# The expert planner of an attention and mixture-of-experts kernel: VectorE's runs on the port shared with GpSimd enter the plan, and the due times are set anew

## The chip, the cores and the metric

One core of a Trainium2 chip. The metric is the device time of one execution in microseconds. Of three runs of the kernel before, the median is 1438.96 us (1438.61 to 1439.52). The profiled execution took 1439.4 us; its span, from the first to the last instruction, is 1437.7 us.

## The reference, cut to what matters

```
scores = q @ k^T / 8                          # 8 batches x 8 heads, 576 x 576, head size 64
keep the 32 largest of each row, softmax, @ v
x = the heads side by side                    # 4608 tokens x 512
logits = x @ w_gate                           # 4608 x 8 experts
for (token, expert) in order of falling logit:
    if token has no expert and expert holds < 576: assign
for each expert e: out[tokens of e] = relu(x @ w1[e]) @ w2[e]    # 512 -> 1024 -> 512
```

Each expert ends with exactly 576 tokens. Which 576 they are is only known when the logits of all tokens are there, so the expert part begins when the attention part has ended.

## The kernel before, in words

`attention` (up to L455) computes x and the logits L, `moe` (L571) the rest. After it comes a check of flags (`redo`), which computes again only what a cheap test finds doubtful; here nothing is computed again.

The expert part handles the experts one after the other, in an order that the data decide: the expert that fills up first is `p` = 0, and so on. For each `p` there are five pieces of work:

- `route(p)` (L637): finds the expert that fills first among those left, and the logit at which it is full. VectorE masks the logits and finds each free token's best expert (L642 to L650). Then six steps: compare all tokens with 32 thresholds (g, L663, in three pieces), count the hits by matmul (L669), fold the counts (cm L673, ch L676), sum (L680), compare with 576 (ok L682), sum (L683), take the highest threshold (mx L688) and make the next thresholds (L694, L695). At the end ei, the expert's number (L699), the positions of its tokens, and, in a chain of its own (L734 to L736), the penalty `pen` and the list U of free tokens that the next routing needs.
- `enlist(p)` (L737): turns the positions into a list of 576 token numbers, idx (L778).
- `weigh(p)` (L779): SyncE loads the expert's w1 and w2 (four transfers of 1 MB, ring of four buffers). They are split into two f16 parts: ScalarE makes the high part in eight chunks (L802), VectorE the rest in sixteen halves, w1l and w2l (L810). There are two sets of split weights.
- `bring(p)` (L825): GpSimd gathers the 576 rows of x by five indirect DMAs (L832), ScalarE and VectorE split each piece into xs (L852, L855), SyncE transposes it into xT (L856). For `p` = 0 TensorE transposes instead (L842). There are two xT buffers and four buffers for gathered rows.
- `ffn(p)` (L857): 16 groups of 12 matmuls for the first product (L872), relu on ScalarE (hh, L881) and its remainder on VectorE (hl, L882); then 108 matmuls of the second product (L896, L899), copies to ob (L906, L908, L910), and five scatters by indirect DMA on GpSimd (L911).

Besides these, `verdict` (L913) does the cheap test: some dozen VectorE instructions on the statistics of the attention part and one matmul.

The order of the instructions on each engine's queue is not the order of this list. Each operation is entered in a `Plan` (L21) with its engine (V, A, G, P for TensorE, D for SyncE's DMA queue), what it waits for, a planned duration `d`, a time `late` from its end to its result, and a due time `t`. `Plan.run` then plays the work through on planned clocks: on each engine, of the operations that could start within `window` of the first that can, it takes the one with the smallest `t`, and among the engines the one that starts first. The instructions are written to the queues in that order, and the chip works each queue strictly in that order, with the waits that the dependences need.

The due times of the expert part are offsets to 47 per expert, in the dictionary at L583: RT is subtracted for `route`, TE added for `enlist` after the routing's end (TE0 for `p` = 0), TN for the chain of `pen` and U, WT and XT are subtracted for weights and x (WT0, XT0 for `p` = 0), WD is the step from one weight chunk to the next, RA and RD are those of relu and its remainder, VD is the verdict's. The `W_` entries are the windows of the engines. `GL` is the planned time from a gather's end to its rows' arrival.

The attention part is ordered by another instance of the same class, with due times and windows of its own (L140).

Of the kernel before, what the change touches and what calls it, by code (L numbers as in the profile page):

```python
# [7 lines left out]
F32 = mybir.dt.float32  # L8
# [12 lines left out]
class Plan:  # L21
# [11 lines left out]

    def at(self, t, f, pre=(), take=None, free=(), e=None, d=0.0, late=0.0, order=(), m=0):

        pre, order = ([p for p in l or () if p is not None] for l in (pre, order))
        op = dict(t=t, f=f, n=len(pre) + len(order), next=[], pre=pre, order=order, take=take, left=0, free=[], e=e, d=d, late=late, m=m)
# [12 lines left out]
    def run(self):  # L50
        clock = {e: 0.0 for e in "VAGPD"}
        ready = {e: [] for e in clock}
        count = mode = 0

        def add(op):
# [6 lines left out]
        def go(op, start):  # L62
            nonlocal count, mode
# [507 lines left out]
def moe(tc, K, L, x, w1, w2, out, marks=None):  # L571
# [4 lines left out]
    with ExitStack() as ctx:  # L576
# [26 lines left out]
        def span(c):  # L603

            Lf=L.rearrange("p t e -> p (t e)")
            def a0():
                R["rng"]=sm.tile([128,2],F32,name="rng"); V.tensor_reduce(R["rng"][:,0:1],Lf,axis=AX.X,op=ALU.min)
            c.add("V",.37,a0)
            c.add("V",.37,lambda: V.tensor_reduce(R["rng"][:,1:2],Lf,axis=AX.X,op=ALU.max))
            c.add("V",.07,lambda: V.tensor_scalar(R["rng"][:,0:1],R["rng"][:,0:1],-1.0,None,op0=ALU.mult))  # L610
# [26 lines left out]
        def route(p,c):  # L637
# [7 lines left out]
            c.add("V",.37,lambda: V.tensor_reduce(o("v",128,NT),D_["ml"],axis=AX.X,op=ALU.max))  # L645
            c.add("V",.37,lambda: V.tensor_tensor(o("oh",128,NT,E),D_["ml"],D_["v"].unsqueeze(2).to_broadcast([128,NT,E]),op=ALU.is_equal))
            c.add("V",.37,lambda: V.tensor_tensor(D_["oh"],D_["oh"],rev.unsqueeze(1).to_broadcast([128,NT,E]),op=ALU.mult))
            c.add("V",.37,lambda: V.tensor_reduce(o("ce",128,NT),D_["oh"],axis=AX.X,op=ALU.max))
            if p: c.add("V",.11,lambda: V.tensor_tensor(D_["ce"],D_["ce"],U,op=ALU.mult))
            c.add("V",.37,lambda: V.tensor_tensor(o("ohb",128,NT,E,dt=BF16),D_["ce"].unsqueeze(2).to_broadcast([128,NT,E]),rev.unsqueeze(1).to_broadcast([128,NT,E]),op=ALU.is_equal))  # L650
            if p<E-1:
                pcs=3 if p==0 else GP; n=NT//pcs
                D_["lo"]=lo0; D_["thr"]=thr0; lowop=None
                for s in range(STEPS):
# [4 lines left out]
                    for q in range(pcs):  # L659
# [10 lines left out]
                        mms.append(plan.at(c.t,count,cv+(mms[-1:]),e="P",d=.026*(n//4) if p else .03*n+.03,m=0 if p else 32))  # L670
                    c.pre=[mms[-1]]; c.t+=.15
                    if p:
                        c.add("V",.10,lambda: V.tensor_tensor(o("cm",128,32),D_["pc"][:,:32],dm,op=ALU.mult))  # L673
# [3 lines left out]
                        c.add("V",.10,fold)  # L677
# [4 lines left out]
                        c.add("V",.07,lambda: V.tensor_scalar(o("ok",128,E,dt=BF16),D_["pn"][:,:E],float(CAP),-1.0/T,op0=ALU.is_ge,op1=ALU.add))  # L682
                        c.add("P",.04,lambda: P.matmul(D_["pn"][:,16:16+E],quart,D_["ok"],start=True,stop=True,skip_group_check=True))  # L683
                    else:
                        def enough(s=s): D_["okb"]=okbs[s%2]; V.tensor_scalar(D_["okb"][:T,:],D_["pn"][:T,:E],float(CAP),None,op0=ALU.is_ge)
                        c.add("V",.07,enough)
                        c.add("P",.04,lambda: P.matmul(D_["pn"][:,16:16+E],onesb[:T+1,:],D_["okb"],start=True,stop=True,skip_group_check=True),m=33)
                    c.add("V",.07,lambda: V.tensor_reduce(o("mx",128,1,bufs=3),D_["pn"][:,16:16+E],axis=AX.X,op=ALU.max),lowop)  # L688
                    st=stp[:,s:s+1]
# [47 lines left out]
        def enlist(p,c):  # L737
# [29 lines left out]
            c.pre=last  # L767
            c.add("V",.25,lambda: V.tensor_tensor(o("oz",128,4,40),D_["po"][:,:160].rearrange("p (j c) -> p j c",j=4),d4.unsqueeze(2).to_broadcast([128,4,40]),op=ALU.mult))
# [3 lines left out]
            c.add("V",.25,gathered)  # L772
            def spread():
# [51 lines left out]
        def bring(p,t):  # L825
# [31 lines left out]
        def ffn(p,t):  # L857
# [3 lines left out]
            for hf in range(2):  # L861
                for f in range(8):
# [18 lines left out]
                    a=plan.at(t+k_*1.45+RA,lambda B=B,f=f,cs=cs: A.activation(e["hh"][0][:,f,cs],B["ph"][:,:288],AF.Relu),[prev],e="A",d=.291)  # L881
                    e["hl"].append(plan.at(t+k_*1.45+RD,lambda B=B,f=f,cs=cs: V.scalar_tensor_tensor(e["hh"][1][:,f,cs],B["ph"][:,:288],0.0,e["hh"][0][:,f,cs],op0=ALU.max,op1=ALU.subtract),[a],e="V",d=.37,free=[tp]))  # L882
            e["lastx"]=prev; plan.frees(prev,e["txT"])
            t2=t+23.2; i_=0
            for j in ((0,1,4,2,3) if JO else range(5)):
# [23 lines left out]
                a=plan.at(t2+i_*.64,put,[prev],e="A",d=.51,take="ob",free=[tp] if j<4 else None); to=a  # L909
                if j==4: a=plan.at(t2+i_*.64+.1,lambda B=B: V.scalar_tensor_tensor(B["ob"][:64],B["po"][:64],OSC,B["o2"],op0=ALU.mult,op1=ALU.add),[a],e="V",d=.6,free=[tp])  # L910
                plan.at(t2+i_*.64+.2,lambda B=B,j=j,n=n: G.indirect_dma_start(out=out,out_offset=bass.IndirectOffsetOnAxis(ap=D_["idx"][:n,j:j+1],axis=0),in_=B["ob"][:n],in_offset=None),[a],e="G",d=1.04,free=[to],late=2.0)  # L911
            plan.frees(prev,e["tW"]); e["mm"]=prev; e["last2"]=prev
        def verdict(c,acc,cuts,flags):  # L913
# [17 lines left out]
            def total():  # L931
                D_=R["pv"]=new(ps,[128,512],F32,"pl",1); P.matmul(D_[:1,:npr+1],onesf[:,0:1],good[:,:npr+1],start=True,stop=True)
            c.add("P",.11,total)
            c.add("V",.1,lambda: V.tensor_tensor(bad[:,:npr+1],want[:,:npr+1],R["pv"][:1,:npr+1],op=ALU.subtract))
            c.add("V",.1,lambda: V.tensor_scalar(bad[:,:npr],bad[:,:npr],bad[:,npr:npr+1],None,op0=ALU.add))
# [59 lines left out]
```

## Time and profile before

| | |
|---|---|
| median of three runs | 1438.96 us |
| profiled execution | 1439.4 us |
| its span | 1437.7 us |
| TensorE busy | 1274.9 us, 89% |
| VectorE busy | 1207.4 us, 84% |
| GpSimd busy | 884.8 us, 62% |
| ScalarE busy | 864.3 us, 60% |
| mean granted TensorE clock | 0.963 of 2.4 GHz |

Times in the rows further down are microseconds from the span's start. PE is TensorE, DVE VectorE, ACT ScalarE, POOL GpSimd, SP SyncE. A row of the timeline has the start, the duration, engine, line, operation, result and source, and in brackets how long the engine was idle before it and what ended the wait. "x5" means that five equal instructions in a row are merged. The granted clock is a share of full speed: 1.00 is 2.4 GHz, 0.50 is 1.2 GHz, and a stretch's value is a mean.

### The profile page before, as it was taken

What the parts mean: (1) busy time and instruction counts of PE and PEld (TensorE: products, weight loads), DVE (VectorE), ACT (ScalarE), POOL (GpSimd) and SP (SyncE); (2) the same over time, 40 slices, a digit from 0 to 9 for tenths busy, and PEclk for the clock granted to TensorE, in tenths of its full rate; (3) what the DMA queues carried; (4) which work ended last, traced back from release to release, by engine and by line L of the source; (5) the groups of instructions that cost most, each with busy time, mean ns of one, the idle gap of its engine ahead of it and who ended that gap; (6) DMA issues with size and microseconds to landing.
All of it is one profiled execution on the core that took longest, in us unless ns stands there. A gap on an engine that the chain in (4) does not pass through costs nothing.

```text
span 1437.7 us, 41210 instructions
## 1 busy us (share of the span) xinstructions
PE 1274.9 (89%) x14803; PEld 907.1 (63%) x14804; DVE 1207.4 (84%) x6007; ACT 864.3 (60%) x1898; POOL 884.8 (62%) x1286
## 2 busy tenths in 40 slices
PE   2889999999999999999999999955989989998996
PEld 1666776776767677776766777643664664664662
DVE  5899999999999999999999999768978878877620
ACT  2677777777777777787777878713334334335420
POOL 5687888798799789879879888601114224223101
PEclk8899999999999999999999999965999999999998
DMA  5434444544345444463445443004347347349411
GB/s 124 89 87 78 111 99 84 109 79 103 78 112 94 87 115 82 89 120 84 87 115 91 80 117 63 13 34 150 132 99 202 125 93 208 132 92 287 115 33 36
DMA packets 293383, 148.45 MB, mean 103 GB/s; under 512 B 250672, under 2 KB 275248, under 8 KB 292144
## 3 DMA queue, kind: packets, MB, share of 16 engines
q1 hardware_dynamic: 287280, 126.84, 38.7%
q0 software_dynamic: 5888, 18.88, 4.2%
q8 instruction: 118, 1.93, 0.6%
q14 instruction: 97, 0.79, 0.2%
HBM read 71.34 MB, written 18.87 MB: 63 GB/s over the span
## 4 chain that ended last, share of the span: by engine, by line
PE 52%; DVE 30%; DMA 7%; ACT 5%; issue 3%; POOL 2%; SPq 0%; ACTq 0%; POOLq 0%; DVEq 0%
PE ph L872 13%; PE pv L367 9%; DVE cd L223 9%; PE s L238 8%; PE s L220 6%; DVE st L242 5%; PE po L896 4%; DMA xg<-x,idx 3%; ACT w L235 3%; PE pt L289 2%; PE pt L288 2%; PE pt L283 2%; DVE s L241 2%; DMA xT<-xs 2%; DVE cd L227 2%
## 5 line engine op out<-in xcount | busy, mean ns | idle before, releaser
L223 DVE MAX8 cd<-s 128x8 f32<-128x96 f32 x1728 | 373.6, 252 | 34.3 <-PE s L220 29.7
L299 POOL TENSOR_TENSOR elm<-F,ehm 128x512 f16<-128x512 f32 x256 | 294.3, 1156 | 8.0
L245 ACT ACTIVATE r<-s,st 128x576 bf16<-128x576 f32 x288 | 212.9, 739 | 106.8 <-PE s L238 71.5
L235 ACT ACTIVATE w<-s,st 128x576 uint16<-128x576 f32 x288 | 213.2, 740 | 80.2 <-DVE st L231 77.2
L911 POOL DMA_INDIRECT out_dram<-ob,idx x40 | 59.5, 1486 | 288.7 <-ACT ob L906 224.8
L242 DVE MAX8 st<-s 128x8 f32<-128x584 f32 x288 | 220.8, 767 | 7.5 <-PE s L238 2.6
L220 PE MATMUL s<-K,Q 128*128 128x512 f16 (+3 forms) x1280 | 193.0, 291 | 27.6 <-DMA Q<-nq 20.1
L872 PE MATMUL ph<-xT,w1h 128*128 128x288 f16 x1024 | 196.2, 289 | 5.4 <-DMA xT<-xs 5.4
L289 PE MATMUL pt<-Q,K 66*128 66x128 f16 (+1 forms) x1280 | 179.1, 216 | 0.0
L288 PE MATMUL pt<-Q,K 128*128 128x128 f16 (+1 forms) x1280 | 178.5, 215 | 0.0
L296 POOL TENSOR_SCALAR ehm<-F 128x512 f16<-128x512 f32 x256 | 156.5, 617 | 32.5 <-ACT F L293 30.1
L220 PEld LDWEIGHTS <-Q 128*128 128x128 f16 (+1 forms) x1280 | 104.8, 103 | 108.2 <-DMA Q<-nq 19.7
L238 PE MATMUL s<-w,off 128*128 128x512 f16 x576 | 132.7, 288 | 38.5 <-DVE s L241 30.3
L293 ACT ACTIVATE F<-pt 128x512 f32<-128x512 f32 x256 | 150.6, 596 | 14.7 <-PE pt L289 7.9
L872 PE MATMUL ph<-xT,w1l 128*128 128x288 f16 x512 | 148.0, 289 | 0.0
L367 PE MATMUL pv<-vt,E 128*64 128x65 f32 (+1 forms) x1024 | 146.8, 257 | 0.3 <-DVE L L418 0.3
L881 ACT ACTIVATE hh<-ph 128x288 f16<-128x288 f32 x128 | 52.5, 410 | 142.1 <-PE ph L872 126.4
L238 PE MATMUL s<-w,back 128*128 128x512 f16 x576 | 118.9, 288 | 20.6 <-DVE st L242 18.3
L288 PEld LDWEIGHTS <-K 128*128 128x128 f16 x1280 | 117.2, 99 | 18.4 <-issue 5.3
L367 PEld LDWEIGHTS <-ehm 128*128 128x128 f16 x2048 | 115.9, 101 | 9.8
L367 PEld LDWEIGHTS pv<-vt,E 128*64 128x64 f32 (+1 forms) x1024 | 113.2, 164 | 13.5 <-issue 3.1
L367 PE MATMUL pv<-vl,ehm 128*128 128x65 f16 x1024 | 120.8, 193 | 0.0
(267 smaller groups left out, 3281.2 us busy)
## 6 DMA issues: line engine op xcount, KB each, us to landing
wr<-in_moe_w_dram SPq DMA_DIRECT2D x32, 1024.0 KB, 8.3
kn<-in_k_dram SPq DMA_DIRECT2D x64, 128.0 KB, 2.4
qn<-in_q_dram SPq DMA_DIRECT2D x64, 128.0 KB, 2.3
vn<-in_v_dram SPq DMA_DIRECT2D x64, 128.0 KB, 2.3
x<-xb SPq DMA_DIRECT2D x8, 1024.0 KB, 4.4
Q<-nq SPq DMA_TRANSPOSE x160, 3.2
kn<-in_k_dram SPq DMA_DIRECT2D x64, 16.0 KB, 2.3
qn<-in_q_dram SPq DMA_DIRECT2D x64, 16.0 KB, 2.1
```

The source lines that it names most:

```text
L220: T.matmul(s_ps[rows,a:b_],P[Q][:,qc],P[K][:,h*576+a:h*576+b_],start=(Q=="Q1"),stop=(Q=="Q2"))
L223: V.max(D["cd"][:,c*8:c*8+8],D["s"][:,576*c//NCH:576*(c+1)//NCH])
L235: A.activation(D["w"],D["s"][:,:576],AF.Sign,bias=P["st"][:,i,32:33],scale=(1+2.0**-21),accum_out=acc[:,col])
L238: T.matmul(D["s"][:,a:b_],by,w[:,a:b_],start=False,stop=True,skip_group_check=True)
L242: def next8(): V.max(P["st"][:,i,24:32],D["s"][:,:584])
L245: A.activation(r,D["s"][:,:576],AF.Relu,bias=P["st"][:,i,31:32],scale=-1.0)
L288: T.matmul(o,K2[:,kb:kb+128],Q1[:,qc],start=False,stop=False,skip_group_check=True)
L289: T.matmul(o,K3[0:66,kb:kb+128],Q2[0:66,qc],start=False,stop=(c==3 and h==sub[-1][0]),skip_group_check=True)
L296: G.tensor_scalar(D["eh"],D["E"],1.0,0.0,op0=ALU.mult,op1=ALU.add)
L299: G.tensor_tensor(el,D["E"],D["eh"],op=ALU.subtract); P["e"][i]=(D["eh"],el)
L367: for m_ in (range(N-1) if part==0 else (N-1,)): T.matmul(out,seq[m_][0],seq[m_][1],start=(m_==0),stop=(m_==N-1))
L872: P.matmul(B["ph"][:,:288],a[:,c,fs],xT[:,b+c,cs],start=(i==0),stop=(i==11))
```

## The change: what it does

Each operation gets a mark `k`: for a VectorE operation, that it uses the SBUF port which VectorE and GpSimd share (true unless set to 0), for a GpSimd operation, that it needs this port (only set for gathers and scatters). The plan keeps `held`, the time at which VectorE's present run on the port ends. A VectorE operation with the mark, or a short one that follows a run closely, extends it. A marked GpSimd operation is planned to start no earlier than `held`. Operations that read PSUM (hl, ob of the short piece, the counts and sums of the routing, the x pieces of `p` = 0) and the reductions get `k=0`; the weight halves, xs, the comparisons g and the rest keep the mark.

Gathers and scatters are planned with 1.25 in place of 1.04, counting with 0.031 in place of 0.026 per four, one PSUM operation with 0.33 in place of 0.25. The verdict's matmul takes its PSUM buffer from the ring `ph` by way of the plan, where it had the buffer `pl` of its own accord. All due times and windows of the expert part are set anew. No instruction is added or removed.

```diff
+    def at(self, t, f, pre=(), ..., m=0, k=None):
...
+        op = dict(..., k=(e == "V") if k is None else k)
...
+        held = 0.0
...
             if op["e"] == "P" and op["m"] != mode: d, mode = d + self.SW, op["m"]
+            if op["e"] == "V" and (op["k"] or (d < 0.3 and start < held + 0.03)): held = start + d
...
+                    if e == "G" and op["k"]: t = max(t, held)
                     can.append((t, op["t"], op))
...
-        O=dict(RT=57.787, TE=29.172, TN=157.485, WT=10.39, XT=280.745, RD=-10.792, GL=2.6, W_V=0.1079, W_A=1.7878, W_G=21213.0764, W_P=0.0, W_D=0.0257, WD0=53.661, WD1=52.071, RA=146.279, WT0=-182.776, TE0=-21.804, XT0=-92.95, VD=388.103)
+        O=dict(RT=1076.532, TE=-466.322, TN=-392.603, WT=381.255, XT=184.721, RD=-1511.888, GL=2.3, W_V=0.1032, W_A=0.1345, W_G=1000.0, W_P=0.0, W_D=56.256, WD0=988.41, WD1=120.646, RA=-141.446, WT0=130.349, TE0=43.583, XT0=-126.197, VD=3177.794)
...
-                        mms.append(plan.at(..., d=.026*(n//4) if p else .03*n+.03, ...))
+                        mms.append(plan.at(..., d=.031*(n//4) if p else .03*n+.03, ...))
...
-                g=plan.at(t+.1*j,lambda j=j: gather(j),[e["idx"]],e="G",d=1.04,take="xg",late=GL,order=[g,prev])
+                g=plan.at(t+.1*j,lambda j=j: gather(j),[e["idx"]],e="G",d=1.25,take="xg",late=GL,order=[g,prev],k=1)
...
-                    e["x"].append(plan.at(t+.1*j+.03,lo,[a],e="V",d=.6,free=[tp]))
+                    e["x"].append(plan.at(t+.1*j+.03,lo,[a],e="V",d=.6,free=[tp],k=0))
...
-                plan.at(t2+i_*.64+.2, <scatter j>, [a],e="G",d=1.04,free=[to],late=2.0)
+                plan.at(t2+i_*.64+.2, <scatter j>, [a],e="G",d=1.25,free=[to],late=2.0,k=1)
...
-                D_=R["pv"]=new(ps,[128,512],F32,"pl",1); P.matmul(...)
-            c.add("P",.11,total)
+                D_=R["pv"]=new(ps,[128,512],F32,"ph",4); P.matmul(...)
+            tv=c.add("P",.11,total,take="ph",m=1)
```

## Rows read from the trace of the kernel before

**Rows 1.** The page's first part: TensorE's busy time, share, instructions.
```profile
PE 1274.9 (89%) x14803; PEld 907.1 (63%) x14804; DVE 1207.4 (84%) x6007; ACT 864.3 (60%) x1898; POOL 884.8 (62%) x1286
```

**Rows 2.** Busy time by stretch, cut at each expert's first L872; granted clock, DMA.
```profile
core 0: us, PE busy (x) PEld busy (x) DVE busy (x) ACT busy (x) POOL busy (x), PEclk, DMA share, GB/s
...
946.50:995.85 49.35, 18.05 (x280) 14.16 (x281) 42.47 (x153) 9.80 (x11) 7.18 (x5) 0.50 0.32 110
995.85:1053.76 57.91, 53.90 (x400) 33.01 (x399) 49.30 (x155) 20.54 (x36) 12.50 (x9) 0.94 0.40 119
1053.76:1109.42 55.66, 51.86 (x395) 31.80 (x395) 46.66 (x150) 20.32 (x36) 14.98 (x10) 0.97 0.54 150
1109.42:1163.47 54.05, 50.19 (x397) 31.60 (x397) 45.41 (x144) 20.78 (x35) 15.78 (x9) 1.00 0.47 140
1163.47:1217.94 54.47, 51.51 (x397) 32.02 (x397) 45.36 (x144) 20.26 (x34) 17.98 (x11) 0.97 0.49 143
1217.94:1272.05 54.11, 51.59 (x398) 32.06 (x398) 45.42 (x144) 19.86 (x34) 16.30 (x10) 0.97 0.50 143
1272.05:1326.12 54.07, 49.35 (x380) 31.39 (x380) 42.67 (x143) 20.85 (x36) 12.58 (x10) 0.98 0.58 183
1326.12:1376.18 50.06, 50.06 (x325) 31.02 (x326) 28.53 (x62) 19.25 (x33) 11.95 (x11) 0.95 0.47 122
1376.18:1423.40 47.22, 47.22 (x313) 29.27 (x311) 8.01 (x17) 9.54 (x21) 4.74 (x5) 1.00 0.08 27
```

**Rows 3.** TensorE's timeline: the first matmuls of experts 6 and 7.
```profile
1326.12 0.64 PE L872 MATMUL ph<-xT,w1h 128*128 128x288 f16 x2 [4.72 <-DMA xT<-xs]
...
1376.18 0.41 PE L872 MATMUL ph<-xT,w1h 128*128 128x288 f16 x2
```

**Rows 4.** TensorE's waits from 995.85 to 1376.18: us in total, times, longest.
```profile
PE pc L669 <- DVE g L663: 8.4, 7, 3.1
PE pc L680 <- DVE ch L676: 7.2, 4, 2.3
PE ph L872 <- DMA xT<-xs: 5.4, 2, 4.7
```

**Rows 5.** VectorE's waits in the same stretch.
```profile
DVE xs L855 <- ACT xs L852: 41.0, 22, 3.8
DVE mx L688 <- PE pc L683: 7.6, 18, 0.6
DVE ok L682 <- PE pc L680: 4.9, 14, 0.5
...
DVE bs L725 <- PE pc L723: 3.1, 5, 0.6
```

**Rows 6.** VectorE's timeline while expert 4's rows are gathered.
```profile
1200.22 3.10 DVE L810 SCALAR_TENSOR_TENSOR w1l<-wr,w1h 128x512 f16<-128x512 f32 x5
1203.23 0.69 DVE L910 SCALAR_TENSOR_TENSOR ob<-po,o 64x512 f32<-64x512 f32 x1
...
1207.31 0.69 DVE L855 SCALAR_TENSOR_TENSOR xs<-xg,xs 128x512 f16<-128x512 f32 x1 [2.70 <-ACT xs L852]
1207.92 0.20 DVE L676 TENSOR_REDUCE ch<-cm 128x8 f16<-128x32 f32 x1
```

**Rows 7.** GpSimd's timeline: gathers of experts 0, 4 and 7.
```profile
986.51 3.01 POOL L832 DMA_INDIRECT xg<-x,idx  x1 [0.31 <-issue]
...
1200.12 4.06 POOL L832 DMA_INDIRECT xg<-x,idx  x1 [1.51 <-DVE idx L778]
...
1353.28 0.96 POOL L832 DMA_INDIRECT xg<-x,idx  x1 [0.30 <-issue]
```

**Rows 8.** VectorE's groups, 1163.47 to 1217.94: busy us, mean ns, idle before.
```profile
L810 DVE SCALAR_TENSOR_TENSOR w2l<-wr,w2h 128x512 f16<-128x512 f32 x9 | 6.0, 679 | 0.0
L810 DVE SCALAR_TENSOR_TENSOR w1l<-wr,w1h 128x512 f16<-128x512 f32 x8 | 5.2, 692 | 0.0
```

**Rows 9.** VectorE's timeline: one instruction of the verdict.
```profile
997.96 0.45 DVE L920 TENSOR_TENSOR vok<-vr,vc 128x288 f32<-128x288 f32 x1
```

**Rows 10.** The line of the transposes (L856): time to landing.
```profile
DMA to landing us min/median/max: 2.7/4.3/6.1
```

More of the change, by code (lines that the diff above doesn't have):

```diff
@@ L32, in __init__, with at @@
         self.ops = []
-    def at(self, t, f, pre=(), take=None, free=(), e=None, d=0.0, late=0.0, order=(), m=0):
+    def at(self, t, f, pre=(), take=None, free=(), e=None, d=0.0, late=0.0, order=(), m=0, k=None):
         pre, order = ([p for p in l or () if p is not None] for l in (pre, order))
-        op = dict(t=t, f=f, n=len(pre) + len(order), next=[], pre=pre, order=order, take=take, left=0, free=[], e=e, d=d, late=late, m=m)
+        op = dict(t=t, f=f, n=len(pre) + len(order), next=[], pre=pre, order=order, take=take, left=0, free=[], e=e, d=d, late=late, m=m, k=(e == "V") if k is None else k)
         for p in pre + order: p["next"].append(op)
@@ L62, in go @@
         def go(op, start):
-            nonlocal count, mode
+            nonlocal count, mode, held
             op["start"] = start
@@ L607, in a0 @@
                 R["rng"]=sm.tile([128,2],F32,name="rng"); V.tensor_reduce(R["rng"][:,0:1],Lf,axis=AX.X,op=ALU.min)
-            c.add("V",.37,a0)
-            c.add("V",.37,lambda: V.tensor_reduce(R["rng"][:,1:2],Lf,axis=AX.X,op=ALU.max))
+            c.add("V",.37,a0,k=0)
+            c.add("V",.37,lambda: V.tensor_reduce(R["rng"][:,1:2],Lf,axis=AX.X,op=ALU.max),k=0)
             c.add("V",.07,lambda: V.tensor_scalar(R["rng"][:,0:1],R["rng"][:,0:1],-1.0,None,op0=ALU.mult))
@@ L644, in route @@
                 D_["ml"]=L; sc=Chain(c.t-5); span(sc)
-            c.add("V",.37,lambda: V.tensor_reduce(o("v",128,NT),D_["ml"],axis=AX.X,op=ALU.max))
+            c.add("V",.37,lambda: V.tensor_reduce(o("v",128,NT),D_["ml"],axis=AX.X,op=ALU.max),k=0)
             c.add("V",.37,lambda: V.tensor_tensor(o("oh",128,NT,E),D_["ml"],D_["v"].unsqueeze(2).to_broadcast([128,NT,E]),op=ALU.is_equal))
             c.add("V",.37,lambda: V.tensor_tensor(D_["oh"],D_["oh"],rev.unsqueeze(1).to_broadcast([128,NT,E]),op=ALU.mult))
-            c.add("V",.37,lambda: V.tensor_reduce(o("ce",128,NT),D_["oh"],axis=AX.X,op=ALU.max))
+            c.add("V",.37,lambda: V.tensor_reduce(o("ce",128,NT),D_["oh"],axis=AX.X,op=ALU.max),k=0)
             if p: c.add("V",.11,lambda: V.tensor_tensor(D_["ce"],D_["ce"],U,op=ALU.mult))
@@ L669, in count @@
                                 for j in range(q*n,q*n+n,4): P.matmul(D_["pc"][:,:32],D_["g"][:,j:j+4,:].rearrange("p a b -> p (a b)"),D_["ohb"][:,j:j+4,:].rearrange("p a b -> p (a b)"),start=(j==0),stop=(j==NT-4))
-                        mms.append(plan.at(c.t,count,cv+(mms[-1:]),e="P",d=.026*(n//4) if p else .03*n+.03,m=0 if p else 32))
+                        mms.append(plan.at(c.t,count,cv+(mms[-1:]),e="P",d=.031*(n//4) if p else .03*n+.03,m=0 if p else 32))
                     c.pre=[mms[-1]]; c.t+=.15
                     if p:
-                        c.add("V",.10,lambda: V.tensor_tensor(o("cm",128,32),D_["pc"][:,:32],dm,op=ALU.mult))
+                        c.add("V",.10,lambda: V.tensor_tensor(o("cm",128,32),D_["pc"][:,:32],dm,op=ALU.mult),k=0)
                         def fold():
@@ L676, in fold @@
                             with nc.allow_low_precision(reason="counts up to 1152"): V.tensor_reduce(D_["ch"],D_["cm"].rearrange("p (j e) -> p e j",e=E),axis=AX.X,op=ALU.add)
-                        c.add("V",.10,fold)
+                        c.add("V",.10,fold,k=0)
                         def total():
@@ L681, in route @@
                         c.add("P",.04,total)
-                        c.add("V",.07,lambda: V.tensor_scalar(o("ok",128,E,dt=BF16),D_["pn"][:,:E],float(CAP),-1.0/T,op0=ALU.is_ge,op1=ALU.add))
+                        c.add("V",.07,lambda: V.tensor_scalar(o("ok",128,E,dt=BF16),D_["pn"][:,:E],float(CAP),-1.0/T,op0=ALU.is_ge,op1=ALU.add),k=0)
                         c.add("P",.04,lambda: P.matmul(D_["pn"][:,16:16+E],quart,D_["ok"],start=True,stop=True,skip_group_check=True))
@@ L685, in enough @@
                         def enough(s=s): D_["okb"]=okbs[s%2]; V.tensor_scalar(D_["okb"][:T,:],D_["pn"][:T,:E],float(CAP),None,op0=ALU.is_ge)
-                        c.add("V",.07,enough)
+                        c.add("V",.07,enough,k=0)
                         c.add("P",.04,lambda: P.matmul(D_["pn"][:,16:16+E],onesb[:T+1,:],D_["okb"],start=True,stop=True,skip_group_check=True),m=33)
-                    c.add("V",.07,lambda: V.tensor_reduce(o("mx",128,1,bufs=3),D_["pn"][:,16:16+E],axis=AX.X,op=ALU.max),lowop)
+                    c.add("V",.07,lambda: V.tensor_reduce(o("mx",128,1,bufs=3),D_["pn"][:,16:16+E],axis=AX.X,op=ALU.max),lowop,k=0)
                     st=stp[:,s:s+1]
@@ L767, in enlist @@
             c.pre=last
-            c.add("V",.25,lambda: V.tensor_tensor(o("oz",128,4,40),D_["po"][:,:160].rearrange("p (j c) -> p j c",j=4),d4.unsqueeze(2).to_broadcast([128,4,40]),op=ALU.mult))
+            c.add("V",.33,lambda: V.tensor_tensor(o("oz",128,4,40),D_["po"][:,:160].rearrange("p (j c) -> p j c",j=4),d4.unsqueeze(2).to_broadcast([128,4,40]),op=ALU.mult),k=0)
             def gathered():
@@ L771, in gathered @@
                 with nc.allow_low_precision(reason="whole numbers up to 71"): V.tensor_reduce(D_["o1"].rearrange("p a b c -> p (a b c)"),D_["oz"].rearrange("p j c -> p c j"),axis=AX.X,op=ALU.add)
-            c.add("V",.25,gathered)
+            c.add("V",.25,gathered,k=0)
             def spread():
@@ L881, in ffn @@
                     a=plan.at(t+k_*1.45+RA,lambda B=B,f=f,cs=cs: A.activation(e["hh"][0][:,f,cs],B["ph"][:,:288],AF.Relu),[prev],e="A",d=.291)
-                    e["hl"].append(plan.at(t+k_*1.45+RD,lambda B=B,f=f,cs=cs: V.scalar_tensor_tensor(e["hh"][1][:,f,cs],B["ph"][:,:288],0.0,e["hh"][0][:,f,cs],op0=ALU.max,op1=ALU.subtract),[a],e="V",d=.37,free=[tp]))
+                    e["hl"].append(plan.at(t+k_*1.45+RD,lambda B=B,f=f,cs=cs: V.scalar_tensor_tensor(e["hh"][1][:,f,cs],B["ph"][:,:288],0.0,e["hh"][0][:,f,cs],op0=ALU.max,op1=ALU.subtract),[a],e="V",d=.37,free=[tp],k=0))
             e["lastx"]=prev; plan.frees(prev,e["txT"])
@@ L909, in ffn @@
                 a=plan.at(t2+i_*.64,put,[prev],e="A",d=.51,take="ob",free=[tp] if j<4 else None); to=a
-                if j==4: a=plan.at(t2+i_*.64+.1,lambda B=B: V.scalar_tensor_tensor(B["ob"][:64],B["po"][:64],OSC,B["o2"],op0=ALU.mult,op1=ALU.add),[a],e="V",d=.6,free=[tp])
-                plan.at(t2+i_*.64+.2,lambda B=B,j=j,n=n: G.indirect_dma_start(out=out,out_offset=bass.IndirectOffsetOnAxis(ap=D_["idx"][:n,j:j+1],axis=0),in_=B["ob"][:n],in_offset=None),[a],e="G",d=1.04,free=[to],late=2.0)
+                if j==4: a=plan.at(t2+i_*.64+.1,lambda B=B: V.scalar_tensor_tensor(B["ob"][:64],B["po"][:64],OSC,B["o2"],op0=ALU.mult,op1=ALU.add),[a],e="V",d=.6,free=[tp],k=0)
+                plan.at(t2+i_*.64+.2,lambda B=B,j=j,n=n: G.indirect_dma_start(out=out,out_offset=bass.IndirectOffsetOnAxis(ap=D_["idx"][:n,j:j+1],axis=0),in_=B["ob"][:n],in_offset=None),[a],e="G",d=1.25,free=[to],late=2.0,k=1)
             plan.frees(prev,e["tW"]); e["mm"]=prev; e["last2"]=prev
@@ L931, in total @@
             def total():
-                D_=R["pv"]=new(ps,[128,512],F32,"pl",1); P.matmul(D_[:1,:npr+1],onesf[:,0:1],good[:,:npr+1],start=True,stop=True)
-            c.add("P",.11,total)
-            c.add("V",.1,lambda: V.tensor_tensor(bad[:,:npr+1],want[:,:npr+1],R["pv"][:1,:npr+1],op=ALU.subtract))
+                D_=R["pv"]=new(ps,[128,512],F32,"ph",4); P.matmul(D_[:1,:npr+1],onesf[:,0:1],good[:,:npr+1],start=True,stop=True)
+            tv=c.add("P",.11,total,take="ph",m=1)
+            c.add("V",.1,lambda: V.tensor_tensor(bad[:,:npr+1],want[:,:npr+1],R["pv"][:1,:npr+1],op=ALU.subtract),free=[tv])
             c.add("V",.1,lambda: V.tensor_scalar(bad[:,:npr],bad[:,:npr],bad[:,npr:npr+1],None,op0=ALU.add))
```

## The prediction

> **What bounds the kernel now.** Read in this order: the page for the span; the busy time of the engines in stretches cut at the first expert matmul (L872) of each expert; what TensorE waited for; what VectorE waited for; then one expert in order of time.
>
> TensorE is busy for 89% of the span [rows 1]. The attention part is planned by its own instance of the planner, in which no GpSimd operation gets the new mark, so its order stays; it fills the span up to 946.5. All that can change is behind that: 49.35 us in which expert 0 is routed, seven stretches of one expert each, 47.22 us of the last expert, and the scatters behind it [rows 2]. The last expert has nothing beside it: 47.2 us is what its matmuls cost. The stretches of experts 0 to 5 take 54.05 to 57.91 us, that of expert 6, beside which little is routed, 50.06. Per stretch I subtract TensorE's idle time (length minus busy) and what the slower clock costs, (1 - granted clock) x length. Idle: 4.01 + 3.80 + 3.86 + 2.96 + 2.52 + 4.72 + 0 = 21.9 us. Clock: 3.5 + 1.7 + 0 + 1.6 + 1.6 + 1.1 + 2.5 = 12.0 us. Left are 50.4, 50.2, 50.2, 49.9, 50.0, 48.3 and 47.6 us, that is the matmuls of an expert and 1 to 3 us of counting for the routing. So **33.9 us** of the expert part is TensorE not working, or working at the lower of its two levels (1.2 GHz) just after it has waited: expert 6's first two matmuls took 0.64 us behind 4.72 us of idleness, the last expert's 0.41 [rows 3].
>
> What TensorE waits for is mostly not data for the expert: 8.4 us for g and 7.2 us for ch, both of the routing, and 5.4 us for xT [rows 4]. TensorE works its queue in order, so a count that waits for VectorE holds the expert matmuls behind it. And VectorE is late because it stands for 41.0 us, 22 times, in front of xs (L855), whose first half ScalarE can't make before the gathered rows are there [rows 5]. One expert in order of time: VectorE runs five weight halves (w1l) back to back from 1200.22, in 3.10 us, then one operation that reads PSUM, then stands 2.70 us before xs, with the next routing step behind it [rows 6]. The gather that xs needs began at 1200.12 and held GpSimd for 4.06 us, where a gather with VectorE quiet takes 0.96 [rows 7]. The difference, 3.10, is exactly the five halves. That is the port which the change counts: the old plan gave every gather 1.04 us, so it placed xs some 3 us too early, ahead of routing that could have run.
>
> At this row a page speaks against the change. The Trainium skill's "SBUF — State Buffer", section "Who interferes with whom", says that VectorE instructions with two SBUF inputs take only the read interface of the shared pair, that descriptor generation seems to need the write interface, and that a lock is held for one instruction. By that the halves would hold a gather not at all, or for one instruction of 0.6 us, and the new mark on them would delay gathers in the plan for nothing. The row disagrees: 3.10 us over five instructions. I go by the row; by the page the sum would be no gain, about 1439.
>
> **The change, part by part.**
>
> *Port in the plan.* No instruction is added or removed. A gather or scatter is planned to start when VectorE's run of port operations ends, and takes 1.25 us. Its cost is nil by itself (0.96 of work and 0.30 of issue on the chip). What it moves is everything that hangs on gathers: ScalarE's and VectorE's x operations come later in their queues. Worth: the 41.0 us of VectorE standing are the source of the waits for g and ch.
>
> *Due times.* For expert 2, in the planner's units, with some 4 added along a routing chain: before, x pieces -187, routing 36, list (enlist) 70, hl 83, weight halves 84 + 52k, pen/U for the next routing 198. After: list -1445, hl -1418, pen/U -1371, routing -982, weight halves -287 + 121k, x pieces -91. So on VectorE the x pieces fall from first to behind routing and the first two weight chunks. Routing would run ahead of the experts, as it may: a routing needs only the previous routing's end and the list two before. Then indices, gathers and transposes of an expert are ready a stretch early, and a late gather stops nobody.
>
> *Is there room on VectorE?* In the stretch from 1163.47 it is busy 45.36 us [rows 2]; of this the weight halves are 11.2 us [rows 8] and xs five times 0.69, 3.4 us [rows 6]. To that come waits that no order removes wholly, for counts, sums and bases from TensorE: (7.6 + 4.9 + 3.1) / 5 stretches = 3.1 us [rows 5]. Together 48.5 us, against TensorE's 49.9. It fits by 1.4 us, so it fits badly: a half of 0.6 us placed in a gap of 0.3 delays the routing, and TensorE's counts with it. The bounds of what stays lost per stretch are 0 (all gaps filled) and 4.8 (as now: 33.9 / 7). I take 1.5 for each of experts 1 to 5, nearer to 0, because the largest wait, for gathered rows, goes: 7.5 us.
>
> *Expert 0's stretch.* Expert 1 is routed beside expert 0's own matmuls, so its indices can't be had a stretch ahead; some stall stays, between 0 and the 7.5 of now (4.01 idle + 3.5 clock). I take 4.2, of which 1.7 is the low clock with which the first expert starts in any order. The verdict moves from due time 388 to 3177. Its eleven longer instructions, of about 0.4 us each (one of them is in [rows 9]: 0.45), some 4.3 us, leave VectorE while expert 1 is being routed. They land where it is free: in the last expert it is busy 8.01 of 47.22 us [rows 2]. If that cover were gone they would cost their 4.3 us. The verdict's matmul takes one of four ph buffers there for a moment: nothing.
>
> *Start of expert 0.* Its second gather took 3.01 us where 0.96 is free [rows 7]; the third, on which the first matmul waits, is behind it. Between 0 and -2.1 us; I take -1.0, as the plan knows of it but has the same weight halves to place.
>
> *Other queues.* On SP the window grows from 0.03 to 56 and weight loads now outrank transposes: four issues may stand before a transpose, and its landing of 2.7 to 6.1 us [rows 10] go towards the upper end: 0 to 3.4 us per expert, hidden while x is a stretch ahead; without that cover it is part of the fourth rival. On GpSimd gathers still go before scatters; a scatter that waits holds an output buffer, of which there are three, so nothing. On ScalarE relu moves up before the later weight chunks: TensorE's ph buffers come free sooner, but no wait for one stands among TensorE's waits [rows 4]: nothing. The remaining planned durations (0.031, 0.33) only shift placements: nothing.
>
> **Sum.** Against the profiled execution's 1439.4 us (span 1437.7 and 1.7 around it; 0.4 above the median of the runs): -33.9 + 7.5 + 4.2 - 1.0 = -23.2, so 1416.2; on the median 1415.8. I say **1416**. A change under 0.2%, 2.9 us, can't be told from none.
>
> **The rivals.**
> 1. *Full recovery.* Routing runs ahead, VectorE fills every gap, only 1.7 us of low clock stays: 1439 - 33.9 + 1.7 - 2.1 = 1405. For: TensorE's work then sets the end, and expert 6's stretch shows 0 idle already. Against: 1.4 us of room per stretch.
> 2. *A new late one.* Gathers are planned rightly, but transposes are still planned to land after 2.4 and land after 4.3 in the median [rows 10]; TensorE waits for xT in place of g. The 15.6 us of waits for g and ch go [rows 4], 1.9 x 4 experts come, and of the clock's 12.0 I count 2 as gained, since TensorE still waits once per expert: 1439 - 15.6 + 7.6 - 2 = 1429. Against: it needs x to stay just in time.
> 3. *Nothing.* The 4.06 us of a gather are its own and not VectorE's holding it, so that the plan pushes gathers back for nothing and the present waits stay: 1436 to 1442. Against: 4.06 - 0.96 = 3.10, the five halves to the hundredth. The rule of the Trainium skill's "SBUF — State Buffer" named above would lead here; the trace so far speaks against it.
> 4. *Slower: weights starve.* Place: VectorE's queue, where routing, list and hl now all stand before chunks 2 and up and before x. If the eight halves of w1 and three x pieces, 11 x 0.6 (3.10 / 5) = 6.6 us, come only after a routing, TensorE waits 6.6 us per expert in place of 4.8: 5 x 1.8 = +9, about 1448. It decides from 4.8 us of waiting per expert on. For: hardly any room. Against: the planner starts a half in any gap over 0.1 us, and once routing is done VectorE has little to do, 28.53 us in expert 6's stretch [rows 2].
>
> **How the numbers follow.** Forecast (1408 to 1426) 0.52; full recovery 0.16; a new late one 0.13; nothing 0.06; slower 0.13. Faster by over 0.2%: 0.52 + 0.16 + 0.13 = 0.81; within 0.2%: 0.06; slower: 0.13. The likeliest is the forecast, 1416. The range reaches from 1402 (full recovery, with 3 us for what the stretches don't show) to 1437, which leaves out the slower case and most of "nothing", under 2 in 10.
>
> **What would show it.** Right: VectorE's waits before xs fall from 41 us to under 15; TensorE's waits for g and ch fall under 6; routing of an expert ends well over 20 us before its first matmul; stretches of 50 to 52 us; verdict instructions past the second expert. Wrong: TensorE waits for w1l, w2l or xT, or stretches stay at 54; also if gathers still take 3 to 4 us and somebody waits for them, or if attention's order has changed.

## The result and the profile after

The changed kernel takes **1418.88 us** (median of 4 runs, 1417.16 to 1419.65), the kernel before in the same comparison 1439.24 (1438.61 to 1441.44): ratio 0.9854, 95% interval [0.9837, 0.9871]. The forecast was 1416.0 with a range of 1402 to 1437.

TensorE's line of the page, against [rows 1]:

```profile
PE 1268.1 (90%) x14803; PEld 906.5 (64%) x14804; DVE 1206.7 (85%) x6007; ACT 861.0 (61%) x1898; POOL 876.6 (62%) x1286
```

It has the same work in less time. Its stretches, cut at the first expert matmul (now L875) of each expert, as in [rows 2]; the columns are the same (stretch, its length, then busy times of TensorE, its weight loads, VectorE, ScalarE and GpSimd, granted clock, DMA share, GB/s). The first is the start, the last that of the last expert:

```profile
946.50:996.81 50.31, 18.41 (x287) 13.91 (x287) 45.42 (x164) 9.81 (x11) 6.81 (x5) 0.51 0.31 108
996.81:1051.98 55.17, 53.09 (x404) 33.02 (x404) 50.99 (x161) 19.58 (x34) 9.15 (x8) 0.96 0.42 125
1051.98:1101.49 49.51, 49.51 (x395) 31.78 (x395) 45.68 (x145) 19.88 (x34) 12.83 (x9) 1.00 0.55 155
...
1200.55:1250.07 49.52, 49.52 (x395) 31.82 (x394) 44.98 (x144) 19.72 (x34) 12.40 (x10) 1.00 0.57 159
1250.07:1304.12 54.05, 49.58 (x373) 31.15 (x372) 45.37 (x147) 21.90 (x36) 19.58 (x10) 0.98 0.67 210
1304.12:1353.83 49.71, 49.71 (x320) 30.85 (x321) 22.42 (x47) 17.74 (x33) 12.45 (x12) 0.95 0.40 102
1353.83:1401.05 47.22, 47.22 (x313) 29.28 (x311) 8.01 (x17) 9.54 (x21) 4.74 (x5) 1.00 0.08 27
```

Experts 1 to 4 now have no idle time on TensorE and the full clock: 49.5 us each, where [rows 2] had 54.05 to 55.66. Against [rows 2] the start is 0.96 longer, expert 0's stretch 2.74 shorter, those of experts 1 to 4 6.15, 4.52, 4.94 and 4.59, of expert 5 0.02, of expert 6 0.35; with the scatters' 0.05 that makes -22.3, the whole change of the span (1437.7 to 1415.4). So nearly all of it lies in four stretches; expert 5's still stands 4.47 us at its end.

Waits from expert 0's first matmul to expert 7's, of TensorE and of VectorE (us in total, times, longest), against [rows 4, 5]:

```profile
PE ph L875 <- DMA xT<-xs: 4.5, 1, 4.5
...
PE pc L683 <- DVE ch L679: 0.6, 1, 0.6
DVE hl L885 <- ACT hh L884: 13.8, 33, 1.0
...
DVE mx L691 <- PE pc L686: 6.7, 12, 0.6
...
DVE xs L858 <- ACT xs L855: 0.8, 2, 0.6
```

VectorE no longer stands before xs (0.8 us, was 41.0), and TensorE's 15.6 us for g and ch are 0.6. What VectorE does instead is shown by its timeline in expert 4's stretch:

```profile
1246.13 0.17 DVE L676 TENSOR_TENSOR cm<-pc,dm 128x32 f32<-128x32 f32 x1
1246.23 0.67 DVE L813 SCALAR_TENSOR_TENSOR w2l<-wr,w2h 128x512 f16<-128x512 f32 x1
1246.83 0.19 DVE L679 TENSOR_REDUCE ch<-cm 128x8 f16<-128x32 f32 x1
1247.20 0.69 DVE L858 SCALAR_TENSOR_TENSOR xs<-xg,xs 128x512 f16<-128x512 f32 x1 [0.18 <-ACT xs L855]
1247.81 0.69 DVE L813 SCALAR_TENSOR_TENSOR w2l<-wr,w2h 128x512 f16<-128x512 f32 x1
1248.41 0.16 DVE L685 TENSOR_SCALAR ok<-pc 128x8 bf16<-128x8 f32 x1
1248.48 1.28 DVE L813 SCALAR_TENSOR_TENSOR w2l<-wr,w2h 128x512 f16<-128x512 f32 x2
1249.68 0.16 DVE L691 TENSOR_REDUCE mx<-pc 128x1 f32<-128x8 f32 x1
```

Between one step of a search and the next (cm, ch, ok, mx) TensorE must answer; weight halves and xs, one or two at a time, fill just these pauses. Before, five halves ran in one piece and VectorE then stood 2.70 us [rows 6]. The gathers, too, are held for less; the first two of expert 5, against the 4.06 us of [rows 7]:

```profile
1233.61 1.78 POOL L835 DMA_INDIRECT xg<-x,idx  x1 [23.09 <-DVE idx L781]
1235.70 1.09 POOL L835 DMA_INDIRECT xg<-x,idx  x1 [0.30 <-issue]
```

### The profile page after: what moved, and what is told of

It reads as the page before. It is cut to its first block, busy times and chain, and to the rows that moved or that the text cites. A ratio compares the mean times of both kernels' runs of the same rounds, so it can differ in the third digit from the quotient of the medians.

```text
span 1415.4 us, 41189 instructions
## 1 busy us (share of the span) xinstructions
PE 1268.1 (90%) x14803; PEld 906.5 (64%) x14804; DVE 1206.7 (85%) x6007; ACT 861.0 (61%) x1898; POOL 876.6 (62%) x1286
## 4 chain that ended last, share of the span: by engine, by line
PE 62%; DVE 27%; ACT 4%; issue 2%; DMA 2%; POOL 2%; SPq 1%; POOLq 0%; ACTq 0%; DVEq 0%
PE ph L875 14%; PE po L899 11%; DVE cd L226 9%; PE pv L370 9%; PE s L241 8%; PE s L223 6%; DVE st L245 5%; ACT w L238 3%; PE pt L292 2%; PE pt L291 2%; PE pt L286 2%; DVE s L244 2%; DVE cd L230 2%; PE po L902 2%; DVE cd L232 1%
## 5 line engine op out<-in xcount | busy, mean ns | idle before, releaser
L875 PE MATMUL ph<-xT,w1h 128*128 128x288 f16 x1024 | 194.7, 289 | 5.1 <-DMA xT<-xs 4.5
L875 PE MATMUL ph<-xT,w1l 128*128 128x288 f16 x512 | 147.9, 289 | 0.0
L835 POOL DMA_INDIRECT xg<-x,idx x40 | 47.3, 1182 | 155.8 <-DVE idx L781 91.3
L241 PE MATMUL s<-w,back 128*128 128x512 f16 x576 | 119.2, 289 | 20.6 <-DVE st L245 18.3
```

The source lines that it names most:

```text
L241: T.matmul(D["s"][:,a:b_],by,w[:,a:b_],start=False,stop=True,skip_group_check=True)
L875: P.matmul(B["ph"][:,:288],a[:,c,fs],xT[:,b+c,cs],start=(i==0),stop=(i==11))
```

## The experiments

Due times are named by their keys in the dictionary. Where no other line is shown, the rest is the changed kernel.

**The port counted, old due times.**
```diff
-        O=dict(RT=1076.532, ..., VD=3177.794)
+        O=dict(RT=57.787, ..., GL=2.3, ..., VD=388.103)
```


> The changed kernel with the due times, windows and verdict time of the kernel before (GL stays 2.3); what is left of the change is the counting of the port and the planned durations. Theory A (the port counted is what takes VectorE away from in front of xs): VectorE's waits before xs fall from 41 us to under 10, the stretches of experts 1 to 4 take 50 to 52 us, time 1420 to 1425. Theory B (the new due times did it, by putting the routing ahead of the x pieces): some 41 us before xs as before, stretches of 54 us, time about 1439.

Measured: 1450.42 us, ratio to before 1.0083 [1.0061, 1.0104]. Neither theory. Waits between the first matmuls of experts 0 and 7:

```profile
PE pl L767 <- DVE bt L763: 8.5, 1, 8.5
...
DVE xs L858 <- ACT xs L855: 27.4, 14, 7.6
DVE ok L685 <- PE pc L683: 12.3, 20, 1.6
...
DVE mx L691 <- PE pc L686: 11.1, 21, 1.2
```

Waits before xs fall by a third only, and VectorE now also stands 23.4 us for ok and mx, which 12.5 us were before [rows 5]: the pauses of the search stay empty. One wait of TensorE for a token list (bt), 8.5 us, comes on top.

**New due times, the port not counted.**
```diff
-                    if e == "G" and op["k"]: t = max(t, held)
+                    pass
```


> The changed kernel without the one line by which a planned gather or scatter waits for VectorE's run of port operations; due times, windows and durations are the new ones. Theory A (the port): VectorE stands 20 to 41 us before xs again, and TensorE waits for the routing, time 1430 to 1439. Theory B (the due times): as the changed kernel, waits before xs under 5 us, time about 1419.

Measured: 1435.81 us, ratio 1.0000 [0.9981, 1.0018], as theory A has it, with 21.4 us before xs, but only 5.7 for ok and mx:

```profile
DVE xs L858 <- ACT xs L855: 21.4, 15, 3.6
```

So neither part brings time alone. By the waits, the times fill the pauses, and the port keeps VectorE from standing before rows that have not come. The planned durations and GL stay new in all runs; what they are worth by themselves was not tried.

**Routing's times back** (RT, TE, TN, TE0 as before), and **routing's times alone** (these four new, all others as before), both with the port counted.

> The changed kernel with the due times of the routing and of the list of tokens (RT, TE, TN, TE0) as before, so that the routing ranks behind the hl pieces and beside the weight halves again; the port stays counted, the x pieces' and halves' times stay new. Theory A (the routing's rank is what the port needs beside it): TensorE waits for g, ch and ok again, 5 us or more in sum, stretches of 51 to 54 us, time 1428 to 1445. Theory B (the rank of halves and x pieces is enough): time under 1422.

> The port counted, and of the new due times those of the routing and the list alone (RT, TE, TN, TE0); all others and the windows as before. Theory A (port and routing's rank are all that counts): time under 1425, waits before xs under 10 us. Theory B (the halves, hl pieces or windows have to fit too): time over 1430.

The first took 1470.25 us, ratio 1.0230 [1.0213, 1.0246], slower than either theory said: TensorE waits 24.7 us for g, ch and ok, and VectorE 42.5 us before xs again. The second took 1436.95, 0.9993 [0.9982, 1.0003]: theory B. So the routing's rank is needed and is not enough. The second is the one in which routing really runs ahead; the indices of experts 5 and 6, and its stretches 1 and 6:

```profile
1220.73 0.17 DVE L781 SCALAR_TENSOR_TENSOR idx<-f 128x5 int32<-128x5 f32 x1
1270.03 0.17 DVE L781 SCALAR_TENSOR_TENSOR idx<-f 128x5 int32<-128x5 f32 x1
```
```profile
1050.08:1106.03 55.95, 52.66 (x415) 33.19 (x413) 51.15 (x171) 19.72 (x34) 13.28 (x11) 0.97 0.51 147
...
1324.87:1371.93 47.06, 47.06 (x314) 29.37 (x313) 17.07 (x33) 16.88 (x29) 5.70 (x6) 1.00 0.09 31
```

Experts 5 and 6 begin at 1271.66 and 1324.87, 50.9 and 54.8 us behind their indices. The lead grows from 18.0 us for expert 1 by 4 to 12 per expert, and VectorE is busy 51.15 of 55.95 us while it does. The stretch of expert 6 is 3.0 us shorter than before, those of experts 1 to 4 are together 3.3 longer [rows 2].

**Times of x and loads back** (XT, XT0, WT, WT0, W_G, W_D).

> The changed kernel with the due times of the x pieces and the weight loads (XT, XT0, WT, WT0) and the windows of GpSimd and SP (W_G, W_D) as before. Theory A (of the forecast: the x pieces must fall behind the routing): VectorE's waits before xs come back, over 10 us, time over 1425. Theory B (with the port counted the x pieces come up in the plan only when their gathers are there, so their rank hardly matters): xs waits under 5 us, time 1415 to 1422.

1418.87 us, 0.9870 [0.9854, 0.9885], 1.0 us before xs: theory B, no difference from the changed kernel.

**Verdict early** (VD=388.103).

> The changed kernel with the verdict's due time VD at its old 388 in place of 3178. Theory A (the verdict's 4.3 us on VectorE compete with the routing of expert 1): the start and the stretch of expert 0 together get 1 to 4.3 us longer, time 1420 to 1423. Theory B (VectorE fills gaps with it): no difference, 1418 to 1420.

1418.37 us, 0.9865 [0.9849, 0.9882]: theory B on the whole. Expert 0 begins at 999.90, 3.1 us later than in the changed kernel, and expert 1 at 1051.02, 0.96 earlier; but the attention part had ended 1.24 us earlier here, so that start and stretch together are 0.3 us longer. The run moves the verdict forward (its eleven longer instructions stand from 984.06 on) and not back to its place before the change, see below.

**The stall before expert 6.** In the changed kernel's SyncE queue weight loads of expert 7 (L793) lie between expert 6's transposes (L859), and TensorE's next matmul waits:

```profile
1289.82 1.34 SPq L859 DMA_TRANSPOSE xT<-xs  x1
1291.43 0.50 SPq L793 DMA_DIRECT2D wr<-in_moe_w_dram  x1
1292.77 8.20 SPq L859 DMA_TRANSPOSE xT<-xs  x2
...
1304.12 0.64 PE L875 MATMUL ph<-xT,w1h 128*128 128x288 f16 x2 [4.47 <-DMA xT<-xs]
```

Transposes issued from 1283 to 1306 take 8.9 us to land (median of 3), those from 1233 to 1250, with no load beside them, 3.1 (median of 4). Three edits on this place: all loads behind the last transpose of the expert before; then in place of that, the last expert's loads behind its own last transpose; then, added to the second, its gathers planned to land 5.0 after their end.
```diff
-  late=2.0+3.0*(k+1),order=ops[-1:]))
+  late=2.0+3.0*(k+1),order=ops[-1:]+(X[p-1]["x"][-1:] if p else [])))
...
+            if p==E-1: o,l=X[p]['x'][-1],X[p]['ld'][0]; l['order'].append(o); l['n']+=1; o['next'].append(l)
...
-  take="xg",late=GL,order=[g,prev],k=1)
+  take="xg",late=GL if p<E-1 else 5.0,order=[g,prev],k=1)
```


> The changed kernel with one more order for SP: the weight loads of an expert are issued behind the last transpose of the expert before it. In the plan only expert 7's loads move, behind expert 6's transposes. Theory A (these loads take the DMA engines while expert 6's transposes are under way): expert 6's transposes land in 2 to 4 us, TensorE's wait of 4.5 us for xT and most of the low clock behind it (1.1 + 2.5 us) go, time 1411 to 1414. Theory B (the transposes are late because VectorE's x pieces are late, or SP's queue is): the wait stays at 3 us or more, time about 1419. If expert 7's weights then come too late, TensorE waits for them before the last expert and the gain is given back there.

> The changed kernel with one more order, for the last expert alone: its first weight load is issued behind its own last transpose (the run with the loads behind expert 6's transposes left the wait for xT, but the loads then fell on expert 7's gathers, and ScalarE stood before xs). Theory A (the loads' traffic is what makes transposes and gathers late): no wait of TensorE over 1 us between expert 1 and the end, stretches 5 and 6 of 49.5 and 47.5 to 49.5 us, time 1409 to 1413, 0.4 to 0.7% under the changed kernel. Theory B (it's lost again elsewhere: expert 7's weights come too late for its first matmul, a wait for w1h or w1l): time 1415 to 1422.

> The kernel whose last weight loads stand behind the last transpose, and in the plan the last expert's gathers land 5.0 in place of 2.3 after their end (in that kernel's trace ScalarE stood 6.24 us before the first xs of the last expert, and TensorE then 2.58 for hl); only two relu pieces move ahead of that xs. Theory A (that standing is what stage 6 still loses): TensorE's wait for hl goes, 2 to 3 us less than that kernel's 1412.3, so 1409 to 1410.5. Theory B (the wait moves to the next xs or to a weight): 1411.5 to 1413.

The first took 1416.23, 0.9851 [0.9835, 0.9868], between its theories: the wait for xT is gone, but the loads, now from 1304.70, lie on expert 7's gathers; ScalarE stands 9.36 us before xs, and TensorE 5.70 for hl. The second took 1412.29, 0.9825 [0.9811, 0.9838], the time of theory A, with a wait of 2.58 for hl left, more than theory A allowed. The third took **1410.26** (1408.71 to 1413.56), 0.9803 [0.9788, 0.9818], by its median its theory A, with 0.5 us left of the wait for hl. It is faster than both kernels of the case; that it is faster than the second (1411.28 to 1413.77) is not shown, as the runs overlap. Its stretches of experts 5 and 6:

```profile
1251.24:1300.73 49.49, 49.49 (x372) 31.13 (x371) 44.71 (x144) 19.69 (x34) 18.97 (x10) 1.00 0.51 153
1300.73:1348.80 48.07, 47.60 (x323) 29.72 (x322) 23.59 (x50) 19.98 (x35) 13.19 (x13) 1.00 0.62 179
```

Together 97.56 us, where the changed kernel has 103.76.

**The port by itself.** VectorE computes indices and goes on with a run of one kind; GpSimd starts a gather when it has the indices.
```python
V.scalar_tensor_tensor(idx, ...)
for z in range(n): V.scalar_tensor_tensor(w[z], wr, 128.0, wh, op0=ALU.mult, op1=ALU.subtract)
G.indirect_dma_start(out=xg, ..., in_offset=bass.IndirectOffsetOnAxis(ap=idx[:,0:1], axis=0))
V.tensor_copy(sink, xg[:,:4])
```


> A kernel of its own, that leaves the whole computation out: VectorE makes indices and goes on without a break with a run of operations of one kind, while GpSimd starts one gather as soon as it has the indices; eight kinds of run and one trial without any, each twice. Theory A (a gather is held until VectorE's unbroken run of operations with SBUF inputs ends): the gather with no run takes 0.9 to 1.1 us; beside 8 weight halves (some 4.9 us) and beside 16 halves of half the size it ends when the run ends, 4.5 to 6 us; beside 8 comparisons as for g likewise; beside 8 operations that read PSUM, and beside reductions, it takes about 1 us; a run of 4 halves, one longer PSUM operation and 4 halves lets it through after the first 4 (about 3 us), with a short PSUM operation between, after all 8 (about 5.5 us), as the change's two lines on held have it. Theory B (a lock for one instruction at a time): beside 8 halves 1 to 1.7 us, beside the smaller ones less. Theory C (operations with two SBUF inputs hold nothing): 0.9 to 1.1 us beside every run but the copies.

> The gather trials again, again with the whole computation left out, but each operation of a run now writes a tile of its own. In the first trials they all wrote the same tile, so each waited for the one before: eight halves took 5.77 us, 0.72 apiece, where five of the kernel's take 3.10, 0.60 apiece, each beginning before the last has ended. One trial (same) keeps the one tile. Theory A (VectorE's operations hold the gather only while they overlap without a break): beside 8 halves of 0.60 apiece the gather takes 4 to 5.5 us and ends about 0.95 us after the run; beside the same halves on one tile 1.15 us again; beside 16 quarters, and 8 comparisons as for g, long too; beside operations that read PSUM or beside reductions about 1 us; with one PSUM operation between 4 and 4 halves it ends 0.95 us after the first 4. Theory B (the gathers' long times in the kernel come from something else on the chip, as traffic of weights): about 1 us beside every run.

> The gather trials a third time, the computation left out again. In the second trials only one of the kinds held its gather (2.95 us, both times), the one in which VectorE had not stood still for some 5 us before its indices; in all others it had just waited for the gather before. Here four halves run ahead of the indices, and behind them what was tried before. Theory A (only a VectorE that has been running without a stop keeps a gather out, until the next operation that is not one with SBUF inputs): without halves ahead (cold) 1.15 us as before; with them, beside 8 halves 4.5 to 5.8 us, with a short PSUM operation after 4 about 3 us, with a longer one or a reduction there about 3 us too; beside 8 comparisons 3 to 4.5 us; beside PSUM operations, reductions and halves on one tile about 1 us. Theory B (it was something else about that one trial): 0.9 to 1.25 us with the halves ahead as without.

First trials: 0.94 to 1.15 us beside every run, which fits theory B best; but each operation there waited for the one before. Second trials: the same, up to 1.22, also beside overlapping halves, against theory A, but 2.95 us both times with a short PSUM operation after four halves, against theory B; of the trials with an overlapping run of SBUF inputs, there alone had VectorE run overlapping halves up to the indices. The third put four halves ahead of the indices of all trials but cold, phal and one without a run. GpSimd's gathers of the third:

```profile
34.33 1.15 POOL L999 DMA_INDIRECT xgcold<-x,idx  x1 [4.58 <-DVE idx L997]
42.34 5.37 POOL L999 DMA_INDIRECT xgwarm<-x,idx  x1 [6.86 <-DVE idx L997]
...
60.65 1.15 POOL L999 DMA_INDIRECT xgwsam<-x,idx  x1 [5.35 <-DVE idx L997]
68.88 5.92 POOL L999 DMA_INDIRECT xgwqua<-x,idx  x1 [7.08 <-DVE idx L997]
80.10 4.30 POOL L999 DMA_INDIRECT xgwcmp<-x,idx  x1 [5.30 <-DVE idx L997]
89.76 0.95 POOL L999 DMA_INDIRECT xgwpsu<-x,idx  x1 [5.36 <-DVE idx L997]
96.09 0.95 POOL L999 DMA_INDIRECT xgwred<-x,idx  x1 [5.38 <-DVE idx L997]
102.48 3.23 POOL L999 DMA_INDIRECT xgwcop<-x,idx  x1 [5.44 <-DVE idx L997]
111.16 2.96 POOL L999 DMA_INDIRECT xgwmxs<-x,idx  x1 [5.46 <-DVE idx L997]
119.44 2.96 POOL L999 DMA_INDIRECT xgwmxl<-x,idx  x1 [5.32 <-DVE idx L997]
...
137.17 1.15 POOL L999 DMA_INDIRECT xgphal<-x,idx  x1 [6.39 <-DVE idx L997]
```

VectorE's eight halves beside the first two, from the same run:

```profile
33.98 4.89 DVE L981 SCALAR_TENSOR_TENSOR wlcold0n<-wr,wh 128x512 f16<-128x512 f32 x8
...
41.99 4.90 DVE L981 SCALAR_TENSOR_TENSOR wlwarm0n<-wr,wh 128x512 f16<-128x512 f32 x8
```

This is theory A. Eight halves (warm; 5.37 us again when repeated, the other kinds were tried once), sixteen of half the size (wqua), eight comparisons (wcmp) and eight copies (wcop) keep the gather out until they end: the halves at 46.89, the gather 0.82 later at 47.71. Operations that read PSUM (wpsu) and reductions (wred) don't. A short PSUM operation after four halves (wmxs) lets it through exactly as a longer one does (wmxl), and halves that each wait for the one before (wsam) hold nothing. Nor does a run hold that began 0.35 us before the gather, behind a pause (cold) or behind PSUM operations (phal).

## Why the prediction came out as it did

**Sum.** The terms against the stretches (idle time plus clock, by the prediction's rule): expert 0's stretch 4.2 forecast, 2.08 + 0.04 x 55.17 = 4.3 measured. Experts 1 to 5: 1.5 each forecast; 0 for four of them, and 4.47 + 0.02 x 54.05 = 5.6 for the fifth, to which come 0.05 x 49.71 = 2.5 of low clock in expert 6's stretch that the forecast counted as gained: 8.1 for 7.5. Start: -1.0 forecast, +0.96 measured. So the sum is close by luck, because two errors cancel: for experts 1 to 4 the first rival came true (TensorE never waits, where 1.4 us of room looked too little), 6.0 us better than forecast, and for expert 5 the stall that comes from transfers stayed, 6.6 us worse. These terms give -33.9 + 8.1 + 4.3 + 1.0 = -20.5; the other 1.8 us lie mostly in what the rule left as TensorE's own work, now 49.5 us in stretches that were left with 49.9 to 50.2.

**Port.** That VectorE's run holds the gather was right: 3.10 us over five halves [rows 6, 7] is what the trials show of eight (5.37). That the difference is the five halves to the hundredth is chance: the gather began 0.10 us before them and ended 0.86 after them, where the trials have 0.82 from the run's end to the gather's. At this row the Trainium skill's "SBUF — State Buffer", section "Who interferes with whom", has operations with two SBUF inputs leave descriptor generation alone, as an inference, and a lock last for one instruction. Halves (5.37) and comparisons (4.30) disagree with the first; that copies hold a gather (3.23) and reductions do not (0.95) agrees with the section, but the copies hold it for all eight of them and not for one.

**The step that failed: "Routing would run ahead of the experts".** It doesn't. In the changed kernel the indices of experts 4 and 5 are made at

```profile
1183.65 0.16 DVE L781 SCALAR_TENSOR_TENSOR idx<-f 128x5 int32<-128x5 f32 x1
...
1233.18 0.15 DVE L781 SCALAR_TENSOR_TENSOR idx<-f 128x5 int32<-128x5 f32 x1
```

16.9 us ahead of their first matmuls at 1200.55 and 1250.07, as for experts 2 and 3; before, expert 4's were made at 1199.68, 18.3 us ahead of 1217.94 [rows 2]. Gathers stay just in time, and the sign "well over 20 us before its first matmul" did not come for experts 1 to 5. What went is the standing: with the port counted the plan puts xs where its rows will be there (it stands 0.8 us before xs in place of 41.0), and with routing first the halves fill pauses that routing has anyway. The forecast's own mechanism, tried in the run with the routing's times alone, brings no time. Why routing keeps its 16.9 us in the changed kernel, although it is ranked early, is open. It is not the times of x and loads: with these put back the lead of experts 1 to 5 is 16.5 to 17.4 us. A candidate that was not tried is hl, which ranks ahead of routing in the changed kernel (for expert 2 -1418 against -982) and behind it in the run with the routing's times alone (83 against -982).

**x pieces.** That they "fall from first to behind routing" was read rightly out of the due times and doesn't matter: 1418.87 with their old times.

**Verdict.** The prediction has its eleven longer instructions leave VectorE while expert 1 is routed. They don't: the instruction of [rows 9], at 997.96 before, stands earlier now,

```profile
994.42 0.45 DVE L923 TENSOR_TENSOR vok<-vr,vc 128x288 f32<-128x288 f32 x1
```

and all eleven lie between 991.12 and 1004.46, beside the routing of expert 1. Only the matmul (1299.42) and the six short instructions behind it came late. So the 4.3 us were never moved away; that expert 0's stretch has 4.3 us of idle time and low clock where 4.2 were forecast is luck, and what shortened the stretch was not tried.

**Start.** The forecast saw only the gather, which did shrink (3.01 [rows 7] to 2.34), but that gains nothing: from expert 0's indices to its first matmul it is 12.25 us, 12.28 before. The indices, in the kernel before and in the changed one, are made at

```profile
983.57 0.16 DVE L778 SCALAR_TENSOR_TENSOR idx<-f 128x5 int32<-128x5 f32 x1
...
984.56 0.15 DVE L781 SCALAR_TENSOR_TENSOR idx<-f 128x5 int32<-128x5 f32 x1
```

so the 0.96 was lost ahead of them: 0.44 in the attention part, which ended that much later in this execution, and the rest in the routing of expert 0. Why that routing takes 0.5 us longer was not tried.

**Expert 6's transposes.** They waited 4.72 us before [rows 3] and wait 4.47 now. The forecast counted them as gone and weighed late transposes as a rival for every expert; it is one expert, by the next one's loads, and each of the three edits took the wait away.

**Slower rival.** Weights starved nowhere: no wait of TensorE for w1h, w1l, w2h or w2l stands among its waits in the changed kernel, and the timeline of expert 4's stretch shows the halves between the steps of the routing. The slow run of the case, 1470 us with the routing's times back, is slow from the other side: there the routing comes late and TensorE waits for it.

## What to carry to other kernels

Of a change that mends a cost model and its due times together, try each alone: here the port alone loses 0.8%, the times alone nothing, and both gain 1.5%. In a chain of short steps that wait for another engine, the work to place there comes in pieces as long as the pause, ranked below the chain. Bulk loads are planned by what lands beside them, not by queue order alone.

## What the runs showed of the hardware

In the trials a GpSimd gather of 0.95 us is held by VectorE only if VectorE already runs operations with SBUF inputs that overlap, without a break, and it ends 0.82 us after such a run; a run that began 0.35 us before the gather held nothing, one that began 2.83 us before it did. An operation that reads PSUM, even one of 0.15 us, or a reduction ends the hold there. The change's line on `held` lets such a short one extend the run, so the plan holds gathers longer than the trials do. The rule is not the whole of it. In the changed kernel VectorE runs without a break from 1236.66, behind a reduction, to 1240.40, and neither of these gathers is held, though the second begins 1.80 us into the run:

```profile
1237.09 1.06 POOL L835 DMA_INDIRECT xg<-x,idx  x1 [0.30 <-issue]
1238.46 0.94 POOL L835 DMA_INDIRECT xg<-x,idx  x1 [0.30 <-issue]
```

A scatter that begins 0.87 us into a run is. What else decides was not tried. This scatter, the longest hold seen in the changed kernel, ends 0.88 us after VectorE's run from 1290.37 to 1299.3:

```profile
1291.24 8.94 POOL L914 DMA_INDIRECT out_dram<-ob,idx  x1 [0.30 <-issue]
```
